# The second block's down projection: its first sub-product, A11 x B11, done as seven half-size products too

## Chip, cores and metric

The kernel runs on one core of one Trainium2 chip. The metric is the device time of one execution in microseconds (us). Three runs of the kernel before gave 714.55, 715.41 and 715.11 us; their median, 715.11 us, is the time to beat. A kernel that is profiled leaves a page and a trace of one further execution.

## The reference, cut to what matters

One layer of attention and one gated MLP run on the same normalised input, and their product is added to the input. All data are bfloat16, with 2048 rows of 1024 numbers.

```
xn   = layernorm(x)
s    = attention(xn; wqkv) @ wo          # 32 heads, 8 keys each, dilation 2
h    = silu(xn @ w1) * (xn @ w3)         # 2048 x 3584
g    = silu(h @ w2)                      # the down projection, 3584 -> 1024
out  = x + s * g
```

The change touches one part of `h @ w2`.

## The kernel before, in words

**Tiles and blocks.** The 2048 rows are worked through in two blocks of 1024 (`b` = 0 and 1; `BL` in the code). A block has two row halves of 512, each cut into four groups `g` of 128 rows. The hidden index f has 28 tiles of 128, kept in `h_sb` (128 partitions, 28 tiles, 1024 rows). A matrix product on TensorE takes a stationary operand of 128x128 (loaded by its own instruction) and a moving operand of up to 512 columns, and adds into one of eight PSUM banks (tiles `mm0` to `mm7`, pool "mm").

**Seven products in place of eight.** Each large product of a block is done in Winograd's form of Strassen's method: the operands are cut in two by two, seven products of quarter size take the place of eight, and VectorE (DVE) makes the sums of the operands and of the results. In the down projection of block `b` (`mlp_down`), A is h (its rows cut into the two row halves, its f index into tiles 0 to 13 and 14 to 27) and B is w2 (its f index cut in the same way, its columns into two times 512). The seven products follow each other in a fixed order:

1. A11 x B11 (`prod(pa[g], g, 0, 0, ...)`, four groups into the four banks `pa`);
2. ACT copies `pa` into four further banks `pb` ("dfork"), while A12 x B21 is added to `pa` (`prod(pa[g], g, 0, 1, ...)`). SiLU of `pa` is a first quarter of the gates ("dg", written to `xs`, and to `h_sb` in block 0);
3. S2 x T2 is added to `pb` (`t2`);
4. S1 x T1 into the four banks `pe`. This product alone is done by seven products of half its size (`product2`, line 1041; its matmuls stand at line 1084 of the profile);
5. S4 x B22, T3 and T4 products, with DVE additions ("dsb", "dsa").

Here S1 to S4 are sums of quarters of h, made by DVE in `mlp_down` ("s1" to "s4", 1792 columns each, one per group); T1 to T4 are sums of quarters of w2, made once at the start of the kernel, kept in DRAM (`t_dram`) and loaded for each block.

**How `product2` works.** It cuts the product's 512 rows in two (m = 0, 1), its 14 f tiles into two times seven (even and odd tiles; `NQ` = 7), and its 512 columns in two times 256 (`HC`). DVE makes four sums of the left operand ("l2s1" to "l2s4") and four of the right ("l2t1" to "l2t4"), each of 1792 columns. TensorE then does 7 products x 2 groups x 7 tiles = 98 matmuls of 256 columns. ACT copies results between PSUM and SBUF ("l2s15", "l2fork", "l2u2"), and DVE adds four results of 256 columns within PSUM ("l2c22", "l2c12", two each). It needs one more slot of the pool "r8" (name "ex").

**Slots and queues.** The pool "r8" has six slots, in which weights and sums take turns. The loads of w2 for products 1 and 2 ("w2", 896 KB each, two for each product) and those of T1 to T4 are issued by SP's queue; a load waits until its slot's last reader is done, and what stands behind it in the queue waits too.

**The order.** The order on each engine is fixed when the program is built: a planner (`Plan`) keeps TensorE's operations in the order of the source and places the others by due times, which it works out backwards from TensorE's order. `plan.soon` moves the due time of operations by name. Each engine does its instructions strictly in that order and waits on semaphores; a late operand holds up everything that is queued behind it on the same engine.

**What lies around the product in block 1.** TensorE does the last steps of the up projection (`up_step`, fb = 13; DVE adds "ua2" and "uh" from PSUM, "um" on SBUF, ACT "sg2"), two groups of product 1, then what is left of that up step (`flush`: eight matmuls of 512 columns that read `xs` a last time), the other two groups of product 1, and product 2. At the same time DVE does the softmax of the fourth attention chunk (`softmax(3)`): three additions "z3" of 1024 float32 columns on data that DMAs bring (`a<-E`), a tree of additions and so on; then the weighted sums of the values (`values(3)`: a<-E,vT, and additions to `qo`), which end before the last output projection (`wo(3)`).

Of the kernel before, what the change touches and what calls it, by code (L numbers as in the profile page):

```python
# [9 lines left out]
BF16 = mybir.dt.bfloat16  # L10
# [199 lines left out]
def kernel(  # L210
# [118 lines left out]
    def tt(name, fn, o, a, b, rd, wr, n, fast, late=0.0):  # L329
        occ = n / (1920.0 if fast else 960.0) + 0.068  # L330
        plan.op(DVE, name, lambda: fn(out=o(), in0=a(), in1=b()), rd, wr, occ, 0.08, late=late)  # L331
# [24 lines left out]
    def dma(eng, name, o, a, rd, wr, kb, late=0.0):  # L356
        e = {SP: nc.sync, POOL: nc.gpsimd, ACT: nc.scalar}[eng]
        occ = {SP: 0.45, POOL: 0.58, ACT: 0.42}[eng]
        plan.op(eng, name, lambda: e.dma_start(out=o(), in_=a()), rd, wr, occ, 0.0, nbytes=kb * 1024, late=late)  # L359
# [18 lines left out]
    def r8v(s, dt=BF16):  # L378
        a = s.ap()
        return a.bitcast(dt) if dt != BF16 else a  # L380
# [597 lines left out]
    def mlp_down(b):  # L978
# [5 lines left out]
        def rhs_load(kind, fh=0, dh=0, t=0):  # L984
            res = []
            for q in range(FH // NQ):
                wt = plan.slot("r8", f"d{kind}")
                dt = FP16 if kind == "t" else BF16
                v = lambda wt=wt, dt=dt: r8v(wt, dt)[:, 0:NQ * CH].rearrange("p (k n) -> p k n", k=NQ)
                if kind == "t":  # L990
                    fs = slice(q, FH, 2) if t == T1 else slice(q * NQ, (q + 1) * NQ)
                    dma(SP, f"t2_{b}{t}{q}", v, lambda fs=fs: t_dram[:, fs, t, :],
                        [("td", i) for i in range(FH)[fs]], [wt, (wt, 0), (wt, 1)], 896)
                else:
                    f = fh * FH + q * NQ
                    dma(SP, "w2", v, lambda f=f: w2_r[:, f:f + NQ, dh * CH:(dh + 1) * CH], [], [wt], 896)
                res.append((wt, [lambda k=k, v=v: v()[:, k, :] for k in range(NQ)]))
            return res

# [38 lines left out]
        def s1_parts(g):  # L1038
            return [("s1 part", g, kk) for kk in range(2)]

        def product2(pe, rhs):

            ex = plan.slot("r8", "ex")
            HC = CH // 2
            I = range(2)
            w = [wt for wt, _ in rhs]
            wv = lambda kk, n: (lambda: r8v(w[kk], FP16)[:, 0:NQ * CH].rearrange("p (k n) -> p k n", k=NQ)[:, :, n * HC:(n + 1) * HC])
            tv = lambda: r8v(ex, FP16)[:, 0:NQ * HC].rearrange("p (k n) -> p k n", k=NQ)
            uv = lambda: r8v(ex, FP16)[:, NQ * HC:2 * NQ * HC].rearrange("p (k n) -> p k n", k=NQ)
            part = lambda m, kk, i: [("s1 part", 2 * m + i, kk)]  # L1050
            if b + 1 == NB:
                rows = [((lambda m, kk: (lambda: s1_q2(m, kk))), uv, lambda m, kk: part(m, kk, 0) + part(m, kk, 1),
                         [(ex, 1), (ex, 2)], 2 * NQ * P)]
            else:
                rows = [((lambda m, kk, i=i: (lambda: s1_q(2 * m + i, kk))), (lambda i=i: uv()[:, :, i * P:(i + 1) * P]),
                         (lambda m, kk, i=i: part(m, kk, i)), [(ex, 1 + i)], NQ * P) for i in I]

            def in_place(x, y, neg, n):

                for r, (a, u, cells, uc, size) in enumerate(rows):  # L1060
                    dst, src = a(*x), u if y is None else a(*y)
                    ry = uc if y is None else cells(*y)
                    pair = (src, dst) if neg else (dst, src)
                    tt(n, sub, dst, pair[0], pair[1], cells(*x) + ry, cells(*x), size, True)

            for a, u, cells, uc, size in rows:
                tt("l2s1", add, u, a(1, 0), a(1, 1), cells(1, 0) + cells(1, 1), uc, size, True)
            in_place((1, 0), (0, 0), True, "l2s3")
            tt("l2t1", sub, tv, wv(0, 1), wv(0, 0), [(w[0], 1), (w[0], 0)], [(ex, 0)], NQ * HC, True)
            tt("l2t3", sub, wv(0, 1), wv(1, 1), wv(0, 1), [(w[1], 1), (w[0], 1)], [(w[0], 1)], NQ * HC, True)  # L1070

            lhs = lambda m, kk, i: ([lambda k=k: s1_q(2 * m + i, kk)[:, k, :] for k in range(NQ)],
                                    part(m, kk, i) + s1_cells(2 * m + i))
            lhu = lambda i: ([lambda k=k: uv()[:, k, i * P:(i + 1) * P] for k in range(NQ)], [(ex, 1 + i)])
            rw = lambda kk, n: ([lambda k=k: wv(kk, n)()[:, k, :] for k in range(NQ)], [(w[kk], n), w[kk]])
            rt = ([lambda k=k: tv()[:, k, :] for k in range(NQ)], [(ex, 0)])

            def p(ps, n, A, B, first=False, mark=()):
                a, ra = A
                c, rc = B  # L1080

                def emit():
                    for k in range(NQ):
                        nc.tensor.matmul(half(ps.ap, n)(), lhsT=a[k](), rhs=c[k](), start=first and k == 0, stop=k == NQ - 1,  # L1084
                                         skip_group_check=True)

                plan.op(PE, "mm2 " + ps.name, emit, ra + rc, [ps] + list(mark), NQ * 0.1092, 0.0)
# [5 lines left out]
            in_place((0, 0), None, True, "l2s2")  # L1093
            tt("l2t2", sub, wv(0, 0), wv(1, 1), tv, [(w[1], 1), (ex, 0), (w[0], 0)], [(w[0], 0)], NQ * HC, True)
            s15 = []
            for i in I:
                s15.append(plan.slot("k2", "l2s15"))
                cp("l2s15", lambda i=i: f32(s15[i]), pe[2 + i].ap, [pe[2 + i]], [s15[i]])
                cp("l2fork", half(pe[i].ap, 0), lambda i=i: f32(s15[i])[:, 0:HC], [s15[i]], [pe[i]], 0.33)
# [5 lines left out]
            in_place((0, 1), (0, 0), False, "l2s4")  # L1105
            tt("l2t4", sub, wv(1, 0), wv(1, 0), wv(0, 0), [(w[1], 0), (w[0], 0)], [(w[1], 0)], NQ * HC, True)
            for i in I:
                p(pe[2 + i], 0, lhs(1, 0, i), rw(0, 1))
                tt("l2c22", add, half(pe[2 + i].ap, 1), half(pe[2 + i].ap, 0), lambda i=i: f32(s15[i])[:, HC:CH],
                   [pe[2 + i], s15[i]], [pe[2 + i]], HC, False)  # L1110
            for i in I:
                p(pe[i], 1, lhs(0, 1, i), rw(1, 1))
                tt("l2c12", add, half(pe[i].ap, 1), half(pe[i].ap, 1), lambda i=i: f32(s15[i])[:, HC:CH],
                   [pe[i], s15[i]], [pe[i]], HC, False)
# [49 lines left out]
        pe, sp5 = [], []  # L1164
        for g in G:
            pe.append(bank(f"de{b}_{g}"))
        steps = product2(pe, rhs1)
        next(steps)
        t2(NST - 1)
        for _ in steps:  # L1170
# [366 lines left out]
```

## Time and profile before

| | |
|---|---|
| runs shown | 714.55, 715.11, 715.41 us; median 715.11 us |
| the profiled execution | 715.77 us, of which its span is 714.0 us |
| busy in the span | TensorE 704.2 us (99%), DVE 661.4 us (93%), ACT 387.6 us (54%), GpSimd 50.6 us (7%) |
| TensorE's granted clock | 1.00 |
| block 1's down projection | begins at 600.70 us of the span |

The profiled execution is 0.66 us above the median. Its span is the stretch from its first instruction to its last; the other 1.77 us lie around it, and nothing in the change touches those. Times below are us from the span's start. In a timeline row the first number is the start, the second how long the merged instructions took from the first one's start to the last one's end, then come engine, line, operation, tiles and count, and in brackets the engine's idle time ahead of it with what ended that wait. An instruction on DVE ends about 0.08 us after the next one has started. About one matmul record in 55 is missing from the trace, so that a count can be one short of the program's.

### The profile page before, as it was taken

Reading aid. Unit: us, or ns where it says so; the run is one execution under the profiler, and the core shown is the slowest. Engines: PE = TensorE matmul, PEld = TensorE weight load, DVE = VectorE, ACT = ScalarE, POOL = GpSimd, SP = SyncE. Lnnn points to the kernel's source line nnn. Section 1 sums busy time; section 2 is a strip of 40 time slices with the busy share of each in tenths; the row PEclk is TensorE's granted clock in tenths of the full one; section 3 lists DMA queues with packets and bytes.
Section 4 is the critical chain, followed back from the end, with each engine's and each line's share of the span. In section 5 each row is a group of like instructions: output and inputs, shape, how many; then the busy total and the mean of one; then the engine's idle time right before and its main releaser. Section 6 shows DMA issues by size and latency. Waiting matters only on the chain.

```text
span 714.0 us, 9421 instructions
## 1 busy us (share of the span) xinstructions
PE 704.2 (99%) x3371; PEld 350.5 (49%) x3426; DVE 661.4 (93%) x894; ACT 387.6 (54%) x662; POOL 50.6 (7%) x103
## 2 busy tenths in 40 slices
PE   8999999999999999999999999999999999999998
PEld 5555544444444444744555554444444444456443
DVE  7899999997999999968799999968999996999986
ACT  7654556675556799324545354657565654422133
POOL 1011100202000000021100000022000001200000
PEclk9999999999999999999999999999999999999999
DMA  9999976659644849794654559776553549629502
GB/s 324 281 373 334 341 246 197 209 155 309 204 150 138 305 156 203 193 265 146 236 166 140 179 199 331 254 260 197 162 197 110 194 156 287 203 82 302 177 22 97
DMA packets 132207, 151.37 MB, mean 212 GB/s; under 512 B 17216, under 2 KB 109248, under 8 KB 127808
## 3 DMA queue, kind: packets, MB, share of 16 engines
q1 hardware_dynamic: 121392, 123.03, 55.1%
q0 software_dynamic: 6112, 26.22, 10.1%
q10 hardware_dynamic: 4656, 1.51, 1.3%
q8 instruction: 27, 0.44, 0.3%
q14 instruction: 20, 0.16, 0.1%
HBM read 106.96 MB, written 32.51 MB: 195 GB/s over the span
## 4 chain that ended last, share of the span: by engine, by line
PE 94%; DMA 4%; SPq 1%; issue 1%; DVE 0%; DVEq 0%
PE mm L322 91%; PE mm L1084 3%; DMA r<-in_A_wqkv_dram 3%; DMA r<-in_B_w_dram 2%; SPq L359 1%; DVE xT L331 0%; DVE k L331 0%; PE mm L347 0%; DVEq L1532 0%; DVEq L331 0%
## 5 line engine op out<-in xcount | busy, mean ns | idle before, releaser
L322 PEld LDWEIGHTS <-r 128*128 128x128 f16 (+1 forms) x2276 | 239.8, 107 | 246.3 <-DMA r<-in_A_wqkv_dram 2.5
L322 PE MATMUL mm<-xs,r 128*128 128x512 f16 x1280 | 295.2, 379 | 0.0
L322 PE MATMUL mm<-xT,r 128*128 128x512 bf16 (+2 forms) x956 | 224.4, 371 | 3.4 <-DMA r<-in_A_wqkv_dram 1.0
L336 ACT COPY k<-mm 128x512 f32<-128x512 f32 x196 | 114.2, 587 | 85.2 <-PE mm L322 75.3
L322 PE MATMUL mm<-r,h_sb 128*128 128x512 bf16 (+1 forms) x694 | 153.5, 379 | 0.9 <-DMA r<-in_B_w_dram 0.3
L322 PEld LDWEIGHTS <-h_sb 128*128 128x128 f16 (+1 forms) x800 | 78.2, 98 | 94.1 <-issue 0.6
L336 ACT COPY mm<-mm 128x512 f32<-128x512 f32 (+1 forms) x93 | 52.0, 562 | 68.4 <-PE mm L322 60.2
L331 DVE TENSOR_TENSOR a<-a,a 128x2048 bf16<-128x2048 bf16 (+1 forms) x68 | 82.5, 1214 | 0.3
L331 DVE TENSOR_TENSOR a<-qo,kT 128x2048 bf16<-128x2048 bf16 x64 | 76.5, 1212 | 0.1
L331 DVE TENSOR_TENSOR h_sb<-mm,k 128x512 bf16<-128x512 f32 x96 | 62.2, 678 | 0.5 <-PE mm L322 0.3
L353 ACT ACTIVATE k<-k 128x512 bf16<-128x512 f32 x56 | 34.8, 630 | 49.9 <-DVE k L331 49.9
L331 DVE TENSOR_TENSOR r<-r,r 128x1024 f16<-128x1024 bf16 (+5 forms) x67 | 55.7, 836 | 0.9 <-DMA xT<-r 0.5
L331 DVE TENSOR_TENSOR k<-mm,k 128x512 f32<-128x512 f32 x72 | 47.8, 680 | 8.3 <-PE mm L322 8.0
L331 DVE TENSOR_TENSOR a<-E,vT 128x2048 bf16<-128x2048 bf16 x42 | 49.9, 1216 | 0.0
L331 DVE TENSOR_TENSOR h_sb<-h_sb 128x512 f16<-128x512 bf16 (+5 forms) x83 | 45.7, 594 | 3.7 <-DMA h_sb<-E 1.8
L331 DVE TENSOR_TENSOR h_sb<-h_sb,k 128x1024 bf16<-128x1024 bf16 x56 | 36.9, 682 | 11.6 <-ACT k L336 11.5
L353 ACT ACTIVATE h_sb<-mm 128x512 bf16<-128x512 f32 x60 | 35.8, 597 | 18.4 <-PE mm L322 18.0
L336 ACT CAST k<-mm 128x512 bf16<-128x512 f32 x56 | 32.7, 586 | 13.1 <-PE mm L322 13.1
L331 DVE TENSOR_TENSOR qo<-qo,a 128x2048 bf16<-128x2048 bf16 x32 | 38.9, 1214 | 0.0
L331 DVE TENSOR_TENSOR a<-a 128x1024 bf16<-128x1024 bf16 (+4 forms) x53 | 33.5, 635 | 2.7 <-DMA a<-E 2.5
L331 DVE TENSOR_TENSOR r<-r 128x1024 f16<-128x1024 bf16 (+2 forms) x36 | 27.6, 788 | 0.0
L359 POOL DMA_DIRECT2D a<-E x24 | 12.5, 526 | 171.8 <-DVE qo L331 88.8
(114 smaller groups left out, 426.7 us busy)
## 6 DMA issues: line engine op xcount, KB each, us to landing
r<-in_B_w_dram SPq DMA_DIRECT2D x42, 512.0 KB, 5.5
s_dram<-r POOLq DMA_DIRECT2D x14, 1024.0 KB, 5.4
r<-t_dram SPq DMA_DIRECT2D x16, 896.0 KB, 6.7
r<-s_dram SPq DMA_DIRECT2D x14, 1024.0 KB, 4.9
r<-in_B_w_dram SPq DMA_DIRECT2D x12, 896.0 KB, 6.3
r<-in_A_wqkv_dram SPq DMA_DIRECT2D x10, 1024.0 KB, 6.6
h_sb<-in_B_w_dram SPq DMA_DIRECT2D x14, 512.0 KB, 9.1
t_dram<-h_sb POOLq DMA_DIRECT2D x14, 512.0 KB, 5.8
```

The lines of the kernel that those rows point to most:

```text
L322: nc.tensor.matmul(cut(ps.ap()), lhsT=lhs[k](), rhs=cut(rhs[k]()), start=(first and k == 0), stop=(last and k == n - 1), skip_group_check= ...
L331: plan.op(DVE, name, lambda: fn(out=o(), in0=a(), in1=b()), rd, wr, occ, 0.08, late=late)
L336: plan.op(ACT, name, lambda: nc.scalar.copy(out=o(), in_=a()), rd, wr, occ, 0.11)
L353: plan.op(ACT, name, lambda: nc.scalar.activation(out=o(), in_=a(), func=ACTF.Silu), rd, wr, occ, 0.11, table="silu")
L359: plan.op(eng, name, lambda: e.dma_start(out=o(), in_=a()), rd, wr, occ, 0.0, nbytes=kb * 1024, late=late)
L1084: nc.tensor.matmul(half(ps.ap, n)(), lhsT=a[k](), rhs=c[k](), start=first and k == 0, stop=k == NQ - 1, skip_group_check=True)
```

## The change

Product 1 of block 1 (`L2B = (1,)`) goes through `product2` as well, called by a new function `product2_p1`. `product2` itself is made general: it is given views of its operands and places for its sums. The four sums of h go to `xs`, which the up projection has finished with by then; the sums of w2 go to a new slot "ex1" of the pool "r8" (two of them) and in place of the loaded weights (two). What was left of the last up step (`flush`) is done after the first four half-size products instead of after two groups. The product for T1 calls the same code through `product2_t1`. In the planner "l2c12" and "l2c22" get a due time that is 300 us earlier, in both products.

```diff
+    L2B = (1,)
...
-                    dma(SP, "w2", v, ..., [], [wt], 896)
+                    dma(SP, "w2", v, ..., [], [wt, (wt, 0), (wt, 1)], 896)
...
-        def product2(pe, rhs):
+        def product2(ps, w, bdt, xa, xc, ya, yc, sa, sc, rows, tdst, names, marks=(None, None)):
...
+            asum(0, add, A(1, 0), A(1, 1))
+            tt(f"{names}t1", sub, T[0][0], wv(0, 1), wv(0, 0), ..., NQ * HC, True)
+            asum(2, sub, A(0, 0), A(1, 0))
+            tt(f"{names}t3", sub, T[2][0], wv(1, 1), wv(0, 1), ..., NQ * HC, True)
...
             for i in I:
-                p(pe[2 + i], 0, lhs(0, 0, i), rw(0, 0), True)
+                p(ps[2 + i], 0, lhs(0, 0, i), rw(0, 0), True)
             for i in I:
-                p(pe[2 + i], 1, lhu(i), rt)
+                p(ps[2 + i], 1, yc(0, i), rt(0))
+            asum(1, sub, Sv(0), A(0, 0))
+            tt(f"{names}t2", sub, T[1][0], wv(1, 1), T[0][0], ..., NQ * HC, True)
...
             yield
             for i in I:
-                p(pe[i], 0, lhs(0, 1, i), rw(1, 0))
-                p(pe[2 + i], 0, lhs(0, 0, i), rw(0, 0), mark=[("pr", 12)] * i)
-                cp("l2u2", half(pe[i].ap, 1), half(pe[2 + i].ap, 0), [pe[2 + i]], [pe[i]], 0.27)
+                p(ps[i], 0, lhs(0, 1, i), rw(1, 0))
+                p(ps[2 + i], 0, yc(1, i), rt(1), mark=[marks[0]] * i if marks[0] else ())
+                cp("l2u2", half(ps[i].ap, 1), half(ps[2 + i].ap, 0), [ps[2 + i]], [ps[i]], 0.27)
+            asum(3, sub, A(0, 1), Sv(1))
+            tt(f"{names}t4", sub, T[3][0], wv(1, 0), T[1][0], ..., NQ * HC, True)
             for i in I:
+                p(ps[2 + i], 0, yc(2, i), rt(2))
+                tt("l2c22", add, half(ps[2 + i].ap, 1), half(ps[2 + i].ap, 0), ..., HC, False)
             for i in I:
+                p(ps[i], 1, yc(3, i), rw(1, 1))
+                tt("l2c12", add, half(ps[i].ap, 1), half(ps[i].ap, 1), ..., HC, False)
             for i in I:
-                p(pe[2 + i], 0, lhs(1, 1, i), rw(1, 0), mark=[("pr", 15)] * i)
+                p(ps[2 + i], 0, lhs(1, 1, i), rt(3), mark=[marks[1]] * i if marks[1] else ())
+
+        def product2_p1(ps, rhs):
+            w = [wt for wt, _ in rhs]
+            xa = lambda m, kk, r: (lambda: h_sb[:, kk * NQ:(kk + 1) * NQ, m * HC:(m + 1) * HC])
+            sv = lambda q: xs[:, q].rearrange("p k n -> p (k n)")[:, 0:NQ * HC].rearrange("p (k n) -> p k n", k=NQ)
...
+                ex = plan.slot("r8", "ex1")
...
+            return product2(ps, w, BF16, xa, xc, ya, yc, sa, sc, [None],
+                            [(tv(0), tc(0)), (tv(1), tc(1)), (None, (0, 1)), (None, (1, 0))], "l1")
...
-        for g in G:
-            if g == 2:
-                flush()
-            pa.append(bank(f"da{b}_{g}"))
-            prod(pa[g], g, 0, 0, rhs, True, BF16)
+        if b in L2B:
+            for g in G:
+                pa.append(bank(f"da{b}_{g}"))
+            steps = product2_p1(pa, rhs)
+            next(steps)
+            flush()
+            for _ in steps:
+                pass
+        else:
+            ...                                  # as before
...
+    plan.soon.update({"l2c12": -300.0, "l2c22": -300.0})
```

In the program as built, what TensorE does differs in product 1 of block 1 alone, where 56 matmuls of 512 columns become 98 of 256. DVE has twelve instructions more there (eight sums of 1792 columns, named "l1s1" to "l1s4" and "l1t1" to "l1t4", and four additions of 256 columns in PSUM), and ACT six more. DVE's order differs from about the ninth step of block 1's up projection on; SP's order differs there in two loads of a softmax, and in the down projection in which w2 load goes to which slot: the first load of product 2 now stands where a T2 load stood.

More of the change, by code (lines that the diff above doesn't have):

```diff
@@ new lines, in product2, with asum @@
+            wv = lambda kk, n, dt=bdt: (lambda: r8v(w[kk], dt)[:, 0:NQ * CH].rearrange("p (k n) -> p k n", k=NQ)[:, :, n * HC:(n + 1) * HC])
+            wc = lambda kk, n: [(w[kk], n)]
+            td = lambda q: (tdst[q][0], tdst[q][1]) if tdst[q][0] is not None else (wv(*tdst[q][1], FP16), wc(*tdst[q][1]))
+            T = [td(q) for q in range(4)]
+            def asum(q, fn, src0, src1):
+                for r in rows:
+                    x, y = src0(r), src1(r)
+                    tt(f"{names}s{q + 1}", fn, sa(q, r), x[0], y[0], x[1] + y[1], sc(q, r), 2 * NQ * P // len(rows), True)
@@ L1079, in p @@
+            rt = lambda q: ([lambda k=k: T[q][0]()[:, k, :] for k in range(NQ)], T[q][1])
+            def p(bank, n, A, B, first=False, mark=()):
                 a, ra = A
@@ new lines, in mlp_down, with product2_t1 @@
+        part = lambda m, kk, i: [("s1 part", 2 * m + i, kk)]
+        def product2_t1(pe, rhs):
+            ex = plan.slot("r8", "ex")
+            HC = CH // 2
+            w = [wt for wt, _ in rhs]
+            uv = lambda: r8v(ex, FP16)[:, NQ * HC:2 * NQ * HC].rearrange("p (k n) -> p k n", k=NQ)
+            tv = lambda: r8v(ex, FP16)[:, 0:NQ * HC].rearrange("p (k n) -> p k n", k=NQ)
+            place = {1: (0, 0), 2: (1, 0), 3: (0, 1)}
+            if b + 1 == NB:
+                rows = [None]
+                xa = lambda m, kk, r: (lambda: s1_q2(m, kk))
+                xc = lambda m, kk, r: part(m, kk, 0) + part(m, kk, 1)
+                sa = lambda q, r: uv if q == 0 else xa(*place[q], r)
+                sc = lambda q, r: [(ex, 1), (ex, 2)] if q == 0 else xc(*place[q], r)
+            else:
+                rows = [0, 1]
+                xa = lambda m, kk, r: (lambda: s1_q(2 * m + r, kk))
+                xc = lambda m, kk, r: part(m, kk, r)
+                sa = lambda q, r: (lambda: uv()[:, :, r * P:(r + 1) * P]) if q == 0 else xa(*place[q], r)
+                sc = lambda q, r: [(ex, 1 + r)] if q == 0 else xc(*place[q], r)
+            ya = lambda m, kk, i: ([lambda k=k: s1_q(2 * m + i, kk)[:, k, :] for k in range(NQ)],
+                                   part(m, kk, i) + s1_cells(2 * m + i))
+            yc = lambda q, i: ([lambda k=k: uv()[:, k, i * P:(i + 1) * P] for k in range(NQ)], [(ex, 1 + i)]) if q == 0 else ya(*place[q], i)
+            return product2(pe, w, FP16, xa, xc, ya, yc, sa, sc, rows,
+                            [(tv, [(ex, 0)]), (None, (0, 0)), (None, (0, 1)), (None, (1, 0))], "l2",
+                            marks=(("pr", 12), ("pr", 15)))
@@ L1166, in mlp_down @@
             pe.append(bank(f"de{b}_{g}"))
-        steps = product2(pe, rhs1)
+        steps = product2_t1(pe, rhs1)
         next(steps)
```

81 lines of the change are left out of this document (37 added, 44 removed).

## The prediction, on record before the result

> **What bounds the kernel now.** I read the page first.
>
> ```profile
> span 714.0 us, 9421 instructions
> PE 704.2 (99%) x3371; PEld 350.5 (49%) x3426; DVE 661.4 (93%) x894; ACT 387.6 (54%) x662; POOL 50.6 (7%) x103
> PE 94%; DMA 4%; SPq 1%; issue 1%; DVE 0%; DVEq 0%
> ```
>
> The second line is each engine's busy time, the third the chain of work that ended last, by engine. TensorE sets the end, so a microsecond off its queue could be a microsecond off the kernel. But DVE is at 93%, and the change pays for TensorE's time with DVE's. So the question is how much room DVE has in this stage. The table of windows has one row for product 1 as it is (sum of all columns: TensorE, weight loads, DVE, ACT, GpSimd):
>
> ```profile
> 600.70:612.90 12.20, 11.82 (x55) 5.33 (x55) 11.32 (x15) 5.85 (x8) 0.00 (x0) 1.00 0.77 237
> ```
>
> DVE is busy 11.32 of 12.20 us, ACT 5.85. Next the timelines, TensorE's first.
>
> ```profile
> 595.52 1.89 PE L322 MATMUL mm<-xs,r 128*128 128x512 f16 x8
> 600.70 1.67 PE L322 MATMUL mm<-r,h_sb 128*128 128x512 bf16 x7
> 602.71 4.69 PE L322 MATMUL mm<-r,h_sb 128*128 128x512 bf16 x21 [0.33 <-DMA r<-in_B_w_dram]
> 607.24 1.89 PE L322 MATMUL mm<-xs,r 128*128 128x512 f16 x8
> 609.18 27.14 PE L322 MATMUL mm<-r,h_sb 128*128 128x512 bf16 x124
> 636.16 1.69 PE L1084 MATMUL mm<-r,xT 128*128 128x256 f16 x14
> 642.24 7.80 PE L1084 MATMUL mm<-r,xT 128*128 128x256 f16 x70
> 649.88 33.40 PE L322 MATMUL mm<-r,h_sb 128*128 128x512 bf16 x152
> ```
>
> Row two is the start of product 1, row four the rest of the up step, and the L1084 rows are T1's half-size products. TensorE has one hole, ahead of row three, where the second w2 load is late. The chain says how late:
>
> ```profile
> 590.77 11.89 DMA r<-in_B_w_dram
> ```
>
> Then DVE, with the waits in brackets.
>
> ```profile
> 593.75 0.69 DVE L331 TENSOR_TENSOR h_sb<-h_sb,k 128x1024 bf16<-128x1024 bf16 x1 [1.67 <-ACT k L336]
> 594.61 0.69 DVE L331 TENSOR_TENSOR h_sb<-h_sb,k 128x1024 bf16<-128x1024 bf16 x1 [0.17 <-ACT k L336]
> 598.38 0.69 DVE L331 TENSOR_TENSOR k<-mm,k 128x512 f32<-128x512 f32 x1 [3.08 <-PE mm L322]
> 600.14 1.23 DVE L331 TENSOR_TENSOR a<-a 128x1024 f32<-128x1024 bf16 x1 [1.06 <-DMA a<-E]
> 601.28 0.69 DVE L331 TENSOR_TENSOR h_sb<-mm,k 128x512 bf16<-128x512 f32 x1
> 605.76 1.48 DVE L331 TENSOR_TENSOR a<-a 128x512 f32<-128x512 f32 x3
> 608.92 0.69 DVE L331 TENSOR_TENSOR h_sb<-h_sb,k 128x1024 bf16<-128x1024 bf16 x1 [0.42 <-ACT k L336]
> 609.78 0.69 DVE L331 TENSOR_TENSOR h_sb<-h_sb,k 128x1024 bf16<-128x1024 bf16 x1 [0.17 <-ACT k L336]
> 610.51 2.09 DVE L331 TENSOR_TENSOR xT<-h_sb 128x1792 f16<-128x1792 bf16 x2
> 613.12 1.08 DVE L331 TENSOR_TENSOR h_sb<-h_sb 128x1792 f16<-128x1792 bf16 x1
> 614.12 0.42 DVE L331 TENSOR_TENSOR a<-a 128x256 f32<-128x256 f32 x1
> 640.18 1.22 DVE L331 TENSOR_TENSOR qo<-qo,a 128x2048 bf16<-128x2048 bf16 x1
> 644.73 1.09 DVE L331 TENSOR_TENSOR xT<-xT 128x1792 f16<-128x1792 f16 x1
> 646.74 0.78 DVE L331 TENSOR_TENSOR mm<-mm,k 128x256 f32<-128x256 f32 x2
> 683.09 1.21 DVE L331 TENSOR_TENSOR qo<-qo,a 128x2048 bf16<-128x2048 bf16 x1
> 689.41 0.69 DVE L331 TENSOR_TENSOR r<-mm,k 128x512 bf16<-128x512 f32 x1 [1.98 <-PE mm L322]
> ```
>
> The row at 610.51 is "s1", the first sum of the later products; 644.73 is "l2s4" of T1's stage. Two things are to be seen. All of DVE's room is ahead of "s1": 1.67 + 0.17 + 3.08 + 1.06 + 0.42 + 0.17 = 6.57 us. From there to the wait of 1.98 us at 689.41 the rows follow each other without a bracket. What DVE cannot fit in before 610.51 it carries for 79 us.
>
> **TensorE's part.** From 607.24 to 636.16 run 8 + 126 matmuls of 512 columns (the 124 records and two that are missing): 28.92 / 134 = 0.2158 us each. From 642.24 to 649.88 run 70 of 256: 0.1091 us each. Product 1 loses 56 x 0.2158 = 12.09 us and gets 98 x 0.1091 = 10.69: 1.40 us less. The hole goes too: without it row three would start at 600.70 + 7 x 0.2158 = 602.21, so it costs 0.50 us; the late w2 load is now first read by TensorE 4.8 us after 600.70, at 605.5, and it landed at 602.66. So TensorE alone could be 1.90 us ahead at the end of product 1.
>
> *A rule against that.* The Trainium skill, page "TensorE: Matmul & The Clock Gate", section "Back-to-back issue gap", gives a stream of weight loads and matmuls 81 ns per matmul at 128 columns and 131 ns at 512, so that halving the columns would save much less than half. As an estimate from that page, even 81 ns would make the 98 matmuls 7.9 us against 7.3 us for the 56, a loss. This trace disagrees: 109.1 against 215.8 ns, almost exactly half, and the sum goes by the trace.
>
> **DVE's part.** Instructions start 0.08 us before the one ahead has ended (613.12 + 1.08 against 614.12). Per instruction that gives 1.00 us for 1792 columns, 1.15 for a z3 addition, 0.61 for 512 columns from PSUM and for "um", 0.35 for 256 columns in PSUM or in float32. Added are 8 x 1.00 + 4 x 0.35 = 9.4 us. They would fit into 6.57 us of waits only in part, and the waits are not all usable: the second sum goes to `xs` rows that the matmuls of the row 595.52 read until 597.3, so "l1s2" runs at about 597.4. The sums "l1s1", "l1t1" and "l1s2" (3 us) are free, in the waits up to 600.14. The rest I walk through in the changed program's order. There the first z3 addition, which waits for a DMA until 600.14, stands ahead of the last up step's four additions from PSUM, and everything after it is back to back:
>
> z3 to 601.28; four PSUM additions to 603.72; "l1t2" 604.72 (its load landed at 602.66); "l1s3" 605.72; z3 606.87; "l1t3" 607.87; z3 609.02; "l1s4" 610.02; a tree step 610.63; "l1t4" 611.63; "l1c22" 611.98; tree 612.33; "l1c22" 612.68; tree 612.88; "um" 613.49; "l1c12" 613.84 and 614.19; softmax difference 615.34; "um" 615.95. So "s1" starts at 615.95 in place of 610.51, 5.4 us later.
>
> Does TensorE wait for any of it? After 28 + 8 + 28 matmuls it wants "l1s3"/"l1t3" at 608.53 (ready 607.9): no. It wants "l1s4" at 610.06 (ready 610.1): no. The last half-size product overwrites what "l1c22" reads, wanted 611.59, done 612.06: 0.45 us. It would end at 613.59, and then A12 x B21 adds to banks that ACT must first copy to `pb`.
>
> ```profile
> 612.24 0.57 ACT L336 COPY mm<-mm 128x512 f32<-128x512 f32 x1
> 649.02 2.05 ACT L336 COPY k<-mm 128x512 f32<-128x512 f32 x4 [3.18 <-DVE mm L331]
> ```
>
> The first copy follows the first "l1c12" (ended 613.9) and takes 0.57 us: TensorE goes on at 614.5, 0.9 us late. ACT's six new copies, of at most about 0.6 us each, lie in its idle half; only this one shows. In the kernel before the same point was at 600.70 + 12.09 + 1.73 + 0.50 = 615.02. Of 1.90 us, 0.5 is left.
>
> **T1's stage.** From there the order moves four value steps (640.18 to 644.73, 4.55 us) behind "l2s4". "l2s4" starts at 615.95 + (644.73 - 610.51) - 4.55 = 645.62 and ends at 646.7. TensorE wanted it 42 half-size matmuls after 642.24, at 646.82; with 0.5 us in hand it wants it at 646.3 and waits 0.4. Now the two "l2c22" stand ahead of "l2t4", which ends at 645.62 + 1.00 + 0.70 + 1.08 = 648.4, against a TensorE that comes at 646.7 + 14 x 0.1091 = 648.2: another 0.2. The stage ends at 648.4 + 1.53 = 649.95 against 649.88. The copies that follow ("dsp", row 649.02) come after the second pair of "l2c12" at 648.7 and are in time at 649.4.
>
> Sum: -1.90 + 0.45 + 0.9 + 0.4 + 0.2 = +0.05, and 649.95 against 649.88 says +0.07; I take +0.1. The span becomes 714.1 us, the execution 715.9 against 715.77, and the median 715.11 + 0.1 = **715.2 us**: the same, as 0.2% (1.43 us) is about what a measurement of this kernel can tell.
>
> **The rest of the kernel.** DVE is then 5.4 us behind. The rows that ask for its work:
>
> ```profile
> 695.20 1.89 PE L322 MATMUL mm<-h_sb,qo 128*128 128x512 f16 x8
> 696.93 5.34 PE L322 MATMUL mm<-h_sb 128*128 128x512 f16 x24
> ```
>
> `qo` is complete at 684.3 and the sums that follow end before 689.41, less 1.98 us of wait, at 687.4. With 5.4 us more that is 692.8, ahead of 696.93. I price this at nothing; the cover is 4 us.
>
> **Bounds of the unknown.** The walk hangs on one time, 600.14, when the DMAs of `a<-E` have landed. SP's queue around them, before:
>
> ```profile
> 586.19 0.37 SPq L359 DMA_DIRECT2D r<-t_dram  x1
> 586.66 0.56 SPq L359 DMA_DIRECT2D vT<-park_v  x1
> 587.33 3.35 SPq L359 DMA_DIRECT2D a<-E  x4
> 590.77 0.53 SPq L359 DMA_DIRECT2D r<-in_B_w_dram  x1
> 591.40 7.66 SPq L359 DMA_DIRECT2D a<-E  x4
> ```
>
> In the changed program the first of these is a w2 load of equal size; the rest stands as it is, and I take the same landing. Every later microsecond goes straight to the end. Every earlier one is gained only until the last PSUM additions can run (their bank is written about 601, so 603.7 could be 601.7) and the late w2 load lands (602.66, read by "l1t2" from 603.7): 1.0 us. So from this -0.9 to, if the cluster lands 1 us later, +1.1.
>
> **Rivals.** *TensorE alone sets the end* (0.06): all its waits vanish because DVE finds time that I do not see, and the time is 715.1 - 1.9 = 713.2. For it speaks the chain with PE 94%; against it the unbracketed DVE rows from 610.51 on.
>
> *The DVE queue is held by a late load* (0.13), on the slower side: the first z3 addition now stands ahead of the up step's PSUM additions, and "l1t2" waits for a w2 load that took 11.89 us, with every later sum queued behind. Where `a<-E` lands at 602.3 or the w2 load at 605.9 in place of 600.14 and 602.66, the walk is 2.2 us later and the time 717.4. It decides against the forecast from 1.3 us of delay on. For it speaks the wait that is in the trace now; against it that nothing in the change puts more into that queue.
>
> *The debt reaches the output projection* (0.03): were DVE another 2 us behind at 692.8 + 4, each further microsecond is lost; 716 to 718. Against it the 4 us of cover.
>
> *Narrow matmuls do not hold half the time* (0.02).
>
> ```profile
> L1084 PEld LDWEIGHTS <-xT 128*128 128x128 f16 x98 | 9.6, 98 | 1.5
> ```
>
> A weight load takes 98 ns beside a matmul of 109 ns, so 11 ns are spare. From 12.09 / 98 = 123 ns each the 98 matmuls cost more than the 56. At 133 ns they cost 13.0 us, TensorE is 0.4 us behind even without the hole, and the time is 715.5 to 716. The trace's 70 matmuls at 109.1 ns speak against it. The rule of the Trainium skill quoted above is this case.
>
> **The numbers.** The forecast has 0.76. Its own range is 715.2 with -0.9 and +1.1, and 0.3 us for the spread of the runs shown: 714.0 to 716.6. That range also holds part of the late-load and narrow cases, and leaves out about 0.2. Faster by over 0.2% needs 1.43 of the 1.90 us: the first rival, 0.07. Slower by over 0.2%: most of the second and third, 0.14. Within: 0.79.
>
> **What would show it.** Right: no TensorE hole at 602; a wait of about 0.9 us on ACT's copy ahead of A12 x B21; DVE's "s1" near 616 and not 610.5; a wait on `xT` of 0.3 to 0.7 us in T1's stage; its end within 0.5 us of 649.9. Wrong: TensorE without a bracket from 600 to 650 (gain kept), or DVE waiting on a DMA past 601 (loss).

## The result, and the profile after

The changed kernel takes 713.43 us (median of 19 runs, 713.03 to 714.47); the kernel before, in 19 runs on the same chip, 714.72 us (714.29 to 715.96). The ratio is 0.9981, with a 95% interval of 0.9974 to 0.9988: about 1.3 us, 0.19%, faster. The forecast was 715.2 us with a range from 714.0, so the time came out below the range. The profiled execution took 713.99 us, its span 712.2 us (before: 715.77 and 714.0).

The page after: span, busy times, and the chain of work that ended last.

```profile
span 712.2 us, 9520 instructions
PE 702.8 (99%) x3413; PEld 354.8 (50%) x3468; DVE 669.3 (94%) x906; ACT 389.4 (55%) x668; POOL 50.6 (7%) x103
PE 98%; DMA 1%; issue 0%; SPq 0%; DVE 0%; DVEq 0%
```

DVE got 7.9 us more to do, and the chain is TensorE's to 98% (before 94%). Only about 2% of it is the change's doing: the late w2 load, 11.89 us of the chain before, is no longer in it. The rest is the load of wqkv in the first 22 us of the kernel, which takes 3% of the chain before, 1% here and 3% again in a second profiled execution of the changed kernel. TensorE's timeline, from product 1's first matmul (line numbers are one higher; the half-size products now stand at L1073; this trace has 3413 matmul records for 3468 weight loads, so that about one in 63 is missing):

```profile
600.58 1.69 PE L1073 MATMUL mm<-r,h_sb 128*128 128x256 bf16 x14
602.11 1.69 PE L1073 MATMUL mm<-r,xs 128*128 128x256 f16 x14
603.64 1.89 PE L323 MATMUL mm<-xs,r 128*128 128x512 f16 x8
607.65 3.98 PE L1073 MATMUL mm<-r,xs 128*128 128x256 f16 x35
611.48 1.69 PE L1073 MATMUL mm<-r,h_sb 128*128 128x256 f16 x14
613.00 21.31 PE L323 MATMUL mm<-r,h_sb 128*128 128x512 bf16 x96
640.23 8.02 PE L1073 MATMUL mm<-r,xT 128*128 128x256 f16 x70
648.09 12.25 PE L323 MATMUL mm<-r,h_sb 128*128 128x512 bf16 x54
```

No row has a bracket. Product 1 and the eight matmuls of the up step among it take 613.00 - 600.58 = 12.42 us, which is 98 x 0.109 + 8 x 0.216 and nothing else. The 70 matmuls at 640.23 take 648.09 - 640.23 = 7.86 us in place of 7.64 before, so 0.22 us of waits stand there. From product 1's first matmul to the end of T1's stage it was 649.88 - 600.70 = 49.18 us and is 648.09 - 600.58 = 47.51: 1.67 us less, which is the saving of 1.40 and the hole of 0.50, less 0.22. The same two points in a second profiled execution of each kernel (before_again, after_again) lie 49.20 and 47.56 us apart. The 1.3 us between the medians are less than these 1.67, but the interval, 0.9 to 1.9 us, holds both. DVE:

```profile
597.33 1.09 DVE L332 TENSOR_TENSOR xs<-xs,h_sb 128x1792 f16<-128x1792 f16 x1 [1.40 <-PE mm L323]
598.34 1.22 DVE L332 TENSOR_TENSOR a<-a 128x1024 f32<-128x1024 bf16 x1
601.87 1.08 DVE L332 TENSOR_TENSOR r<-r,r 128x1792 f16<-128x1792 bf16 x1
607.14 1.08 DVE L332 TENSOR_TENSOR xs<-h_sb,xs 128x1792 f16<-128x1792 bf16 x1
611.55 0.76 DVE L332 TENSOR_TENSOR mm<-mm,k 128x256 f32<-128x256 f32 x2
614.06 2.09 DVE L332 TENSOR_TENSOR xT<-h_sb 128x1792 f16<-128x1792 bf16 x2
643.74 1.08 DVE L332 TENSOR_TENSOR xT<-xT 128x1792 f16<-128x1792 f16 x1
644.74 0.79 DVE L332 TENSOR_TENSOR mm<-mm,k 128x256 f32<-128x256 f32 x2
```

The first row is "l1s2", the second the first z3 addition, on which the forecast's walk hung. It has no bracket: it starts as soon as "l1s2" lets it, at 598.34, and the forecast had it wait for a DMA until 600.14. The third is "l1t2", the fourth "l1s4", the fifth the two "l1c12", the sixth "s1", the seventh "l2s4". What changed ahead of them is in the table of transfers: the loads that SP issued from the one ahead of vT to the first four of `a<-E` (columns: what, queue, count, KB each, median us from issue to landing), with the first four that GpSimd's queue (POOLq) had under way beside them; first before, then after.

```profile
vT<-park_v SPq DMA_DIRECT2D x1, 1024.0 KB, 11.1
r<-t_dram SPq DMA_DIRECT2D x1, 896.0 KB, 4.6
a<-E SPq DMA_DIRECT2D x4, 64.0 KB, 10.6
a<-E POOLq DMA_DIRECT2D x4, 64.0 KB, 8.4
```

```profile
vT<-park_v SPq DMA_DIRECT2D x1, 1024.0 KB, 9.8
r<-in_B_w_dram SPq DMA_DIRECT2D x1, 896.0 KB, 5.6
a<-E SPq DMA_DIRECT2D x4, 64.0 KB, 9.1
a<-E POOLq DMA_DIRECT2D x4, 64.0 KB, 6.5
```

The load ahead is a T2 load from `t_dram` in the one and a w2 load in the other. It has the same size, and the w2 load takes a microsecond longer by itself; still, what stands behind it takes 1.3 to 1.5 us less, and the transfers of GpSimd's queue, which have a queue of their own, take 1.9 us less. So it is not their place in SP's queue alone that holds transfers up. In the trace the last of the four `a<-E` landed at 599.72 before and at 597.59 after, and the second w2 load at 602.66 and 600.36.

### The profile page after: what moved, and what is told of

It is laid out like the page before. It is cut to its first block, busy times and chain, and to the rows that moved or that the text cites. A ratio compares the mean times of both kernels' runs of the same rounds, so it can differ in the third digit from the quotient of the medians.

```text
span 712.2 us, 9520 instructions
## 1 busy us (share of the span) xinstructions
PE 702.8 (99%) x3413; PEld 354.8 (50%) x3468; DVE 669.3 (94%) x906; ACT 389.4 (55%) x668; POOL 50.6 (7%) x103
## 4 chain that ended last, share of the span: by engine, by line
PE 98%; DMA 1%; issue 0%; SPq 0%; DVE 0%; DVEq 0%
PE mm L323 93%; PE mm L1073 5%; DMA r<-in_A_wqkv_dram 1%; SPq L360 0%; PE mm L502 0%; DVE xT L332 0%; PE mm L348 0%; DVEq L1582 0%; DVEq L332 0%
## 5 line engine op out<-in xcount | busy, mean ns | idle before, releaser
L323 PE MATMUL mm<-r,h_sb 128*128 128x512 f16 (+1 forms) x638 | 141.3, 379 | 0.5
L323 PEld LDWEIGHTS <-h_sb 128*128 128x128 f16 (+1 forms) x744 | 72.7, 98 | 86.8
L332 DVE TENSOR_TENSOR r<-r,r 128x1024 f16<-128x1024 bf16 (+6 forms) x70 | 59.1, 850 | 1.2 <-DMA r<-in_A_wqkv_dram 0.4
L332 DVE TENSOR_TENSOR r<-r 128x1024 f16<-128x1024 bf16 (+3 forms) x37 | 28.8, 800 | 0.0
```

What stands on the lines that cost most here:

```text
L323: nc.tensor.matmul(cut(ps.ap()), lhsT=lhs[k](), rhs=cut(rhs[k]()), start=(first and k == 0), stop=(last and k == n - 1), skip_group_check= ...
```

## The experiments

Theory: the forecast's walk through DVE is right and only its first time was wrong, because the T2 load holds up the transfers behind it more than the w2 load does. Rivals: the landing is chance of one execution; TensorE alone sets the end and DVE has room that does not show. In all experiments but e_nosoon and e_both the order of every queue is held but for what is named: the edit is made after the planner has placed everything, or changes only a layout or what one operation does.

**The same two kernels, profiled again.**

> The kernel before once more, for its trace alone. If the loads of `a<-E` land late in this kernel as a rule, the last SP load of `a_0` lands at 599.7 us within 0.4, the first z3 addition waits for it and starts at about 600.1, the second w2 load of product 1 lands at about 602.7 and TensorE's hole of 0.5 us ahead of row three is there again. If the landing is chance of one execution, these times move by over 1 us and the hole changes with them.

> The changed kernel once more, for its trace alone. If its loads land early as a rule: last SP load of `a_0` at 597.6 us within 0.4, no wait of DVE on a DMA, first z3 addition at about 598.3 right behind the second l1 sum, TensorE without a hole from 600.6 to 648 but for about 0.2 us of waits in T1's stage. If it is chance, the landing moves by over 1 us, and where it lies past 598.3 the end of T1's stage moves with it, one for one.

Times 714.88 and 713.5 us. In before_again all of this part lies 0.9 us earlier, so that the landing came at 598.39 us and not at the 599.7 that was named; the absolute times therefore do not compare from one execution to the next. Measured against product 1's first matmul, the last of the four loads (they fill the tile `a_0`) landed 0.98 and 1.41 us ahead of it in the two executions before, and 2.99 and 2.55 us ahead in the two after; DVE waited for `a<-E` before (0.63 us this time) and not after; the hole was there again before (0.52 us). The spread within a kernel is 0.4 us, the difference between their means 1.6 us. With two executions of each kernel that speaks against chance, and the next experiments bear it out.

**The T2 load put back in front (e_t2first), and in front of nothing (e_hole).**

```diff
-        for o in self.simulate():
+        order = self.simulate()
+        x, y = at[(1, "w", 1, 0, 0, 1)], at[(1, "t", 0, 0, 3, 0)]     # e_t2first, from the changed kernel
+        x, y = at[(1, "w", 0, 0, 0, 1)], at[(1, "t", 0, 0, 3, 0)]     # e_hole, from the kernel before
...
+        order[i], order[j] = order[j], order[i]                       # the two loads, with their buffers
+        for o in order:
             o.emit()
```

> The changed kernel with the load that stands ahead of vT and `a<-E` in SP's queue exchanged for the first T2 load (from t_dram), as it stood in the kernel before; the w2 load that stood there goes to that one's place at 605 and is read from about 614.5. Every other instruction keeps its place. Theory (the source of that load makes the queue behind it slow): last `a_0` load at 599.7, first z3 addition at 600.1, DVE 1.8 us later down to the sum of l2s4, TensorE waits about 1.4 us for ACT's copy ahead of A12 x B21 and 0.4 more in T1's stage, 713.4 + 1.8 = 715.2 us. Rival (the source does not matter, the queue drains faster for another reason): landing 597.6, 713.4 us. Rival (DVE has room that does not show): landing late and still 713.4.

It took 714.86 us; ratio to before 0.9998 (0.9990 to 1.0007). The gain is gone. Transfers, DVE, ACT and TensorE of e_t2first (L333 is the large products, L1084 the half-size ones, L342 DVE, L347 ACT):

```profile
vT<-park_v SPq DMA_DIRECT2D x1, 1024.0 KB, 11.5
r<-t_dram SPq DMA_DIRECT2D x1, 896.0 KB, 4.6
a<-E SPq DMA_DIRECT2D x4, 64.0 KB, 10.9
```

```profile
599.32 1.23 DVE L342 TENSOR_TENSOR a<-a 128x1024 f32<-128x1024 bf16 x1 [1.64 <-DMA a<-E]
```

```profile
612.99 2.04 ACT L347 COPY mm<-mm 128x512 f32<-128x512 f32 x4 [4.76 <-DVE mm L342]
```

```profile
599.84 1.69 PE L1084 MATMUL mm<-r,h_sb 128*128 128x256 bf16 x14
611.21 1.69 PE L1084 MATMUL mm<-r,h_sb 128*128 128x256 f16 x14 [0.24 <-DVE mm L342]
613.62 21.31 PE L333 MATMUL mm<-r,h_sb 128*128 128x512 bf16 x98 [0.71 <-ACT mm L347]
645.86 3.35 PE L1084 MATMUL mm<-r,xT 128*128 128x256 f16 x28 [0.28 <-DVE xT L342]
649.05 6.21 PE L333 MATMUL mm<-r,h_sb 128*128 128x512 bf16 x28
```

The last `a_0` load landed 0.91 us ahead of product 1's first matmul. DVE waits for `a<-E` again, and every wait of the forecast appears in its place: ahead of the last half-size product on "l1c22", ahead of A12 x B21 on ACT's copy, in T1's stage on "l2s4" and once more behind it. The brackets count a part of each; from the starts of the matmuls the waits are 0.40, 0.88, 0.44 and 0.12 us, where the forecast had 0.45, 0.9, 0.4 and 0.2 (another 0.07 us, on "l1s4", were not in it). Product 1 takes 613.62 - 599.84 = 13.78 us, 1.36 more than in the changed kernel (the forecast said 0.45 + 0.9 = 1.35), and T1's stage ends 649.05 - 599.84 = 49.21 us after the first matmul, against 49.18 before: 0.03 us more, where the forecast had 0.07. Of the eleven runs three lie at 713.5 to 713.6 and the others at 714.4 to 715.4; whether the loads landed early in those three is not known, as a run without a profile shows no landing.

> The kernel before with two loads of equal size exchanged in SP's queue, each in the other's place and buffer: product 1's second w2 load now goes first (at 586.2) and the first T2 load, which nobody reads before 620, goes where it stood (590.8); every other instruction keeps its place in its queue. The hole ahead of row three was 0.50 us, so TensorE is 0.5 us ahead and nothing behind it is late: 714.72 - 0.5 = 714.2, ratio 0.9993. Were the hole hidden anyway, 714.7. For the landing: if it matters whether the load in front reads w2 or the t_dram scratch, the last `a_0` load lands at about 597.6 as in the changed kernel; if not, at 599.7 as before.

It took 714.31 us, before 714.77; ratio 0.9995 (0.9986 to 1.0004), as expected in size, though the interval holds no change too. The last `a_0` load landed 2.56 us ahead of the first matmul, as in the changed kernel, and T1's stage ended 649.59 - 600.90 = 48.69 us after it, 0.5 us earlier than before. TensorE's row in product 1 shows the hole gone:

```profile
600.90 6.21 PE L332 MATMUL mm<-r,h_sb 128*128 128x512 bf16 x28
```

**No load in front, and the T2 load in long runs.**

```diff
+        order.remove(x)                                               # e_nofront: x the w2 load in front
+        order.insert(order.index(y), x)                               # y the first T2 load
...
-    t_dram = dram.tile([P, FH, 4, CH], FP16, name="t_dram")           # e_t2flat: e_t2first, and this
+    t_dram = dram.tile([P, 4, FH, CH], FP16, name="t_dram")
...
-                    dma(SP, ..., v, lambda fs=fs: t_dram[:, fs, t, :],
+                    dma(SP, ..., v, lambda fs=fs: t_dram[:, t, fs, :],
```

> The changed kernel with the load ahead of vT and `a<-E` moved out, back to just before the first T2 load at 605. One look at the landings: vT and the loads behind it have the queue for themselves. If bytes alone set the landing, 0.9 MB less at some 300 bytes per ns is 3 us earlier: last a_0 load at 594.6, second w2 load at 597.4. If vT is slow by itself and only hides behind a w2 load, the last a_0 load stays within 1 us of 597.5. The time stays at 713.4, since the second l1 sum holds DVE until 598.3 in any case.

The last `a_0` load landed at 594.48 us, the second w2 load at 598.50; the one run took 713.19 us, inside the range of the changed kernel's runs. With nothing in front vT took 7.3 us, so vT is not slow by itself. The last `a_0` load landed 5.27 us ahead of product 1's first matmul, 2.3 to 2.7 us sooner than in the changed kernel, and that brought nothing that one run could show: DVE was held by "l1s2" as before.

> e_t2first with the t_dram scratch laid out so that the seven tiles of a T2, T3 or T4 load lie side by side: 7 KB runs for each partition in place of seven runs of 1 KB, 4 KB apart (the T1 loads and the stores stay in runs of 1 KB). Every queue keeps its order. If the strided 1 KB pieces of the t_dram load are what holds up vT and the `a<-E` loads behind it, the last a_0 load lands 2.5 to 3 us ahead of product 1's first matmul, as with a w2 load in front (0.9 to 1.4 us with the T2 load in front), TensorE's waits of 0.24, 0.71 and 0.28 us go and the time is 713.4. If it is the place that is read, or the scratch as such, the landing and the waits stay: 714.9.

It took 713.62 us; ratio 0.9982 (0.9974 to 0.9991). The gain is back, with the T2 load in front:

```profile
vT<-park_v SPq DMA_DIRECT2D x1, 1024.0 KB, 9.4
r<-t_dram SPq DMA_DIRECT2D x1, 896.0 KB, 4.4
a<-E SPq DMA_DIRECT2D x4, 64.0 KB, 8.6
```

```profile
600.05 1.69 PE L1084 MATMUL mm<-r,h_sb 128*128 128x256 bf16 x14
612.48 21.32 PE L333 MATMUL mm<-r,h_sb 128*128 128x512 bf16 x98
647.57 7.72 PE L333 MATMUL mm<-r,h_sb 128*128 128x512 bf16 x35
```

The load takes about as long as in e_t2first (4.4 and 4.6 us), but vT behind it 9.4 in place of 11.5 us; the last `a_0` load landed 3.38 us ahead of the first matmul, even sooner than was expected, and TensorE's three waits are gone (647.57 - 600.05 = 47.52 us). The new layout holds for every load of T2, T3 and T4, but this is the only load of `t_dram` that was under way then.

> The kernel before, nothing changed but the layout of the t_dram scratch (7 KB runs for each partition in the T2, T3 and T4 loads, as in e_t2flat). Every queue keeps its order. If the 1 KB pieces of the T2 load held up the queue here too, vT and `a<-E` land some 2 us earlier, the second w2 load lands at about 600.4 us (it landed at 602.7) and TensorE's hole of 0.5 us goes: 714.8 - 0.5 = 714.3 us. DVE's first z3 addition no longer waits, and that is worth nothing here. If the layout matters only beside the changed kernel's loads: hole and time as before, 714.8.

In the kernel before, the long runs close the hole (the last `a_0` load 4.21 us ahead of the first matmul, the second w2 load 0.37 us ahead of it, and 28 matmuls in 6.21 us), but the time is 714.67 us against 714.79, ratio 1.0003 (0.9993 to 1.0012). T1's stage ended 48.68 us after the first matmul, 0.5 earlier; the layout also changes every other T load, and TensorE had 0.17 us of wait in block 0 (ahead of 287.12) in that execution, where the kernel before had 0.08. In the stage, then, the hole's 0.5 us is there in both experiments. In the time it is not shown: e_hole has 0.5 us and e_flat0 0.1, neither beyond its interval.

**DVE's room.**

```diff
+            if names == "l1":                                         # e_sum1: the third sum twice
+                op.emit = lambda: [one() for _ in range(2)]
...
-    plan.soon.update({"l2c12": -300.0, "l2c22": -300.0})              # e_nosoon
...
-    L2B = (1,)                                                        # e_both
+    L2B = (0, 1)
```

> The changed kernel with one of product 1's sums (the third, l1s3, 1.00 us) done twice in a row; same result, every queue else unchanged. Theory (DVE has just enough room: in the changed kernel ACT's first copy is done 0.41 us before TensorE asks for it, l2s4 is already 0.06 and l2t4 0.16 us late): l1c22 makes TensorE wait 0.36 us, ACT's copy makes it 0.6 us late in all at A12 x B21, and T1's stage ends a whole 1.0 us later: 713.4 + 1.0 = 714.4 us. Rival (TensorE alone sets the end, DVE has room): 713.4 us, no new wait.

It took 714.72 us; ratio 0.9998 (0.9990 to 1.0006), 1.3 us more than the changed kernel. T1's stage ended 651.94 - 603.15 = 48.79 us after the first matmul, 1.28 later than in the changed kernel. DVE was later by as much: the repeated sum took 1.13 us and not 1.00, and the first z3 addition began 0.17 us later against the first matmul. TensorE:

```profile
616.50 21.31 PE L323 MATMUL mm<-r,h_sb 128*128 128x512 bf16 x96 [0.71 <-ACT mm L337]
648.75 3.35 PE L1077 MATMUL mm<-r,xT 128*128 128x256 f16 x28 [0.27 <-DVE xT L332]
```

The new waits stand where they were expected. The one on "l1c22" was smaller than said (0.05 us, from the starts of the matmuls) and the one on ACT's copy larger (0.88, of which the bracket counts 0.71). That TensorE alone sets the end is refuted here: DVE's room was used up to within half a microsecond.

> The changed kernel without its last line, which gives the additions l2c22 and l2c12 an earlier due time (both products' additions carry these names). In DVE's order l1c12 then comes behind a softmax difference, and two more value steps (1.14 us each) stand ahead of l2s4, with all four additions behind l2t4. Theory: product 1 stays as it is but for 0.1 us (first ACT copy 0.5 us later, 0.41 spare); l2s4 ends at 744.8 + 2.2 less 100, that is 647.0 where TensorE asks at 644.8; T1's stage ends about 2.1 us later: 713.4 + 2.1 = 715.5 us, slower than before by 0.1%. Rival (TensorE alone): 713.4 us.

It took 715.64 us; ratio 1.0014 (1.0006 to 1.0023), 0.14% slower than before. "l2s4" and TensorE's waits:

```profile
645.40 1.11 DVE L332 TENSOR_TENSOR xT<-xT 128x1792 f16<-128x1792 f16 x1
```

```profile
613.33 21.31 PE L323 MATMUL mm<-r,h_sb 128*128 128x512 bf16 x96 [0.86 <-ACT mm L337]
646.56 3.23 PE L1073 MATMUL mm<-r,xT 128*128 128x256 f16 x28 [1.26 <-DVE xT L332]
```

The size was right, not all of the place: TensorE waited 1.0 us for ACT's first copy, not 0.1. Against product 1's first matmul the first "l1c12" came 0.76 us later (0.23 of it from the first z3 addition on), and ACT then had a softmax exponential of 1.06 us to finish first, which put the copy off by another 0.6. In T1's stage two value steps now stand ahead of "l2s4", and TensorE waited 1.4 us for it. The sums in product 1 pay only in the order that this one line gives DVE: the additions (four in each of the two products) early, and "l2s4" ahead of these value steps.

> The changed kernel with the first block's product 1 done as seven half-size products too. TensorE saves another 1.40 us there (no hole to win: its matmuls of that product stand back to back). In the kernel before, DVE has no wait at all from 225 to 309 us and then 2.3 + 1.2 + 1.4 + 0.8 us up to 322. Theory (DVE has just enough room only where its waits are): the 9.4 us of sums find no wait before 309, about 3.6 us of the debt are left at 322 and TensorE waits for most of what it saved, or more: 713 to 717 us, no clear gain over 713.4. Rival (TensorE alone sets the end): 713.4 - 1.4 = 712.0 us.

It took 718.63 us; ratio 1.0058 (1.0046 to 1.0071), beyond the range that was expected. TensorE in block 0:

```profile
257.75 0.92 PE L1073 MATMUL mm<-r,h_sb 128*128 128x256 bf16 x7 [0.98 <-ACT mm L337]
261.87 3.22 PE L1073 MATMUL mm<-r,xs 128*128 128x256 f16 x28 [0.91 <-ACT mm L337]
341.29 1.89 PE L323 MATMUL mm<-r,qo 128*128 128x512 bf16 x8 [1.81 <-ACT mm L337]
```

These are waits on ACT's copies, which there stand behind other work of ACT's (statistics of a layer norm, table loads, an exponential), so the reason that was expected, DVE's debt, is not what these rows show. From the starts of the matmuls they are 1.15, 1.07 and 1.97 us. Block 1's part also took 2.2 us longer than in the changed kernel (653.51 - 603.76 = 49.75 us from product 1 to the end of T1's stage). Together that is 6.4 of the 6.6 us by which the time exceeds the 712.0 us of TensorE alone. The planner placed everything anew in this kernel, so not every wait can be put down to the sums alone.

**Is there more to be had?** In e_early product 1's second w2 load takes the place in front, and "l1t2" moves into the 1.40 us of DVE's wait; e_flatall adds the long runs and puts "l2t4" ahead of the two "l2c22".

```diff
+        order[i], order[j] = order[j], order[i]                       # the two w2 loads
+        order.remove(t2)
+        order.insert(order.index(s2), t2)                             # l1t2 ahead of l1s2
...
+        order.remove(t4)
+        order.insert(order.index(s4) + 1, t4)                         # e_flatall: l2t4 behind l2s4
```

> The changed kernel with the first two w2 loads behind the front of SP's queue exchanged (each in the other's place and buffer), so that product 1's second w2 load lands at about 591.5 in place of 600.4, and with l1t2 moved in DVE's order ahead of l1s2, into the 1.40 us in which DVE waits for TensorE there. Nothing else moves. Theory: all of DVE's work from l1s3 on is 1.0 us earlier, the 0.22 us of waits in T1's stage go, and as TensorE then waits for nothing the time falls by just that: 713.2 us. Rival (DVE still sets the end): 712.4 us. Rival (the a<-E loads now land later since the small load order changed): 713.4 or more.

The label e_best is the same kernel as e_early.

> e_early once more, for one look: whether its 0.22 us wait in T1's stage stands again (l2t4 behind the two l2c22). 713.2 to 713.6 us.

> e_early with that layout, and with l2t4 ahead of the two l2c22 in T1's stage, which is what its last wait of 0.22 us hung on. Theory: TensorE has no wait left from 600 to 650 and ends T1's stage 47.3 us after product 1's first matmul (47.5 in the changed kernel, 49.2 before): 713.2 us, 0.2 under the changed kernel, the floor of TensorE's own queue here. Rival (the last additions now come late for TensorE's next matmuls): 713.4 to 713.9 us.

They took 713.58 us (0.9981, 0.9972 to 0.9990), 713.9 us in the one further execution of e_early, and 713.54 us (0.9979, 0.9971 to 0.9988). In e_early "l2t4" stayed behind the two "l2c22", so that TensorE's 0.22 us in T1's stage stood in both executions, against what had been expected (47.52 us each from the first matmul to the stage's end). Of the 1.0 us that "l1t2" gave back, DVE lost half in a new wait for TensorE:

```profile
609.38 0.43 DVE L347 TENSOR_TENSOR mm<-mm,k 128x256 f32<-128x256 f32 x1 [0.51 <-PE mm L1089]
```

In e_flatall TensorE's last wait in the stage is gone, to the hundredth as worked out (649.11 - 601.82 = 47.29 us):

```profile
601.82 1.69 PE L1093 MATMUL mm<-r,h_sb 128*128 128x256 bf16 x14
641.47 7.81 PE L1093 MATMUL mm<-r,xT 128*128 128x256 f16 x70
649.11 6.21 PE L342 MATMUL mm<-r,h_sb 128*128 128x512 bf16 x27
```

In the time that is not to be seen: none of these kernels is shown to beat the changed one.

## Why the prediction was wrong, by its own steps

**TensorE's part: right.** 98 half-size matmuls take 0.109 us each, and the hole is gone: 1.90 us ahead at 613.00 (12.42 us where 56 x 0.2158 + 1.73 + 0.50 = 14.3 stood). The rule of the Trainium skill that spoke against it (page "TensorE: Matmul & The Clock Gate", section "Back-to-back issue gap") gives 131 ns at 512 columns for a stream of weight loads and matmuls. The trace has 216 ns at 512 columns and 109 at 256, and it decided rightly. The rival of narrow matmuls falls.

**DVE's walk: right but for its anchor.** From the first z3 addition to "s1" the forecast had 615.95 - 600.14 = 15.81 us; the trace has 614.06 - 598.34 = 15.72. From "s1" to "l2s4" 29.67 and 29.68 us. Only the beginning was 1.80 us off, and all that followed from it: "s1" at 614.06 and not 615.95, no wait on "l1c22", none on ACT's copy (done 0.4 us before TensorE comes), 0.06 us on "l2s4" in place of 0.4. The wait on "l2t4" behind the two "l2c22", said to be 0.2, is there with 0.16.

**The step that failed** is the sentence "the rest stands as it is, and I take the same landing". The load ahead was taken for another of equal size; it reads from another place in another pattern, and what stands behind it lands 1.6 us sooner. e_t2first puts the T2 load back in front, and the stage ends 0.03 us later than before: with the landing it assumed, the forecast's sum of +0.07 was right, and so was "the same". e_t2flat keeps the T2 load in front and changes its pattern, and the gain is back.

**The bound was too narrow for the same reason.** A cluster landing earlier was priced at 1.0 us at most, since the late w2 load was held at 602.66. But that load stands in the same queue and came 2.3 us sooner with the rest (600.36). Two unknowns that hang on one queue were bounded as if only one could move. With both free, the earliest start was the end of "l1s2", 598.3, which gives 715.2 - 1.8 = 713.4. That this is the measured time to a tenth is partly luck: the 715.11 us that the forecast stood on was the median of three runs, and from the 714.72 us of nineteen the same sum gives 713.0.

**The rivals.** *TensorE alone sets the end* gave 713.2 and had 0.06: the time was close to it, but not its reason. The time that DVE gained came from the landing and was not hidden in its own order: one sum of DVE's done twice costs 1.3 us (e_sum1), and DVE's order without the early additions costs 2.2 us (e_nosoon). *A late load holds DVE's queue* was the right mechanism with the wrong sign: it had been holding it before, and the change let it go. *The debt reaches the output projection*: it does not; no wait of TensorE on DVE stands behind 650 us.

**What would show it.** "TensorE without a bracket from 600 to 650 (gain kept)" was named as the sign of a wrong forecast, and it is what the trace shows.

## What to carry to other kernels

When a change puts another transfer into a queue, ask what stands behind it, and whether it reads in the same pattern, not only whether it has the same size; and let everything that lands from that queue move together when bounding it. A walk through one engine's order can be exact to 0.1 us and still be wrong by its first time, so its anchor deserves a range of its own: from what it waits for down to the instruction ahead of it. Extra sums on a second engine are free only as long as the additions and copies that the first engine waits for stand early in the order of whoever makes them, and that has to be seen in each place anew: the same edit in the other block lost 5 us.

## What was not expected of the hardware

A load's reading pattern can cost more in the transfers beside and behind it than in the load itself. The T2 load of 896 KB, in runs of 1 KB read 4 KB apart, with 56 KB from one partition to the next, landed after 4.6 us, a microsecond sooner than the w2 load of equal size (5.6 us; runs of 1 KB too, 256 KB apart, with 2 KB from one partition to the next). vT of 1024 KB behind the T2 load took 11.1 to 11.5 us (three executions), behind the w2 load 9.7 to 10.2 (eight). With the same 56 KB between partitions but runs of 7 KB the T2 load took 4.4 us, and vT 8.9 and 9.4 in two kernels; with nothing in front vT took 7.3. In e_both vT took 11.1 us with a w2 load in front; there that load and vT were both issued before the load ahead of them had landed. GpSimd's transfers were slower beside the T2 load as well, 8.4 us in place of 6.5. So neither the run of 1 KB alone nor the 56 KB alone does it; whether it is the 4 KB from run to run, or the short runs together with the 56 KB, these runs do not tell. The Trainium skill (page "DMA: Bandwidth & Descriptors", section "Specifications") asks for transfers of at least 512 B for full rate. The T2 load itself agrees with it, 4.6 us in short runs against 4.4 in long ones; the 2 us between vT behind the one and behind the other are not in that rule.
